# Another order of TensorE's steps in a segmented memory-transformer kernel

## The chip, the core and the metric

The kernel runs on one core of one Trainium2 chip. The metric is the device time of one execution in microseconds (us); lower is better. The core has five engines with a queue of instructions each: TensorE (PE in the profile, PEld for its loads of stationary operands), VectorE (DVE), ScalarE (ACT), GpSimd (POOL) and SyncE (SP). They run their queues in order and meet only at semaphores.

## The reference

Four layers stand one behind the other on a sequence of 2048 rows of 512 numbers: A, B, A, B, each added to its own input after a normalisation of the rows.

```
def _A_ref(x, mem0, Wq, Wk, Wv, Wo, seg_len):      # 32 heads of 128, 8 memory rows, segments of 32 rows
    mem = mem0
    for s in range(64):
        h = concatenate([mem, x[32 s : 32 s + 32]])  # 40 rows
        q, k, v = h @ Wq, h @ Wk, h @ Wv
        p = softmax(mask(q @ k.T * scale))
        o = (p @ v) @ Wo
        mem = o[:8]                                  # carried into the next segment
        outs.append(o[8:])

def _B_ref(x, wqkv, wo):                            # linear attention, 32 heads of 16
    q, k, v = x @ wqkv
    kv, z = phi(k).T @ v, sum(phi(k))
    return (phi(q) @ kv / (phi(q) @ z)) @ wo

x = x + A(layernorm(x)); x = x + B(layernorm(x))
x = x + A(layernorm(x)); x = x + B(layernorm(x))
```

Layer A is a recurrence: the eight memory rows that leave segment s enter segment s + 1, so the 64 segments of a layer can't be computed side by side. Layer B sums over all rows before any row of its result can be formed.

## The kernel before

The weights of A lie in SBUF throughout. The work is cut into 14,006 steps. A step is one call of `add` (line 1635): an engine, a function that issues one or more instructions, and the steps that it must wait for. Each step has a name made of layer, segment and part, and a count within the part, for example segment 46's `mem0`, step 5.

The parts of a segment s of layer A are these.

- `kq0`, `kq1`, `v` (function `project`, line 2125): the projections. One step of a part is one quarter of the contraction for two outputs: eight matmuls with 512 moving columns each, four at a time side by side in four column groups of TensorE. The second four use the stationary operand that the first four loaded (`again`, line 2038), so such a step is 8 matmuls and 4 weight loads. There are four steps to a part. They are the long products.
- Steps 4 to 7 of `kq0` and `kq1`: copies out of PSUM by ACT or DVE, and transposes by DVE (`turned`, line 2155).
- `mem0`, `mem1` (line 2224): the scores (steps 0 and 1 on TensorE), their exponential (ACT), two maskings (DVE), the sums (step 5, TensorE), a logarithm and an exponential (ACT), the product with v (step 8, TensorE, 20 matmuls) and the scaling (DVE), for the eight memory rows.
- `out` (lines 2373 and 2405): the output projection of the segment, eight steps of eight matmuls with 256 columns, each with its own weight load (line 2387); then a copy and an add.
- `next` (line 2410): the new memory rows are brought into the layout of the next segment, two small steps on TensorE and one copy. This closes the loop of the recurrence.
- `x` (line 2299): the attention of the 32 rows of the segment, with many small TensorE steps (step 1, steps 12 to 15 and 18 to 21); it isn't on the path of the recurrence, and runs while later segments go on.
- `res` (line 2437): moves of result rows by DMA from the queues of POOL and SP (`x_move`, line 1938) and the residual add.

Every four segments the parts `prep`, `left0`, `left1`, `leftv` and `lefts` (lines 2166 and 2207) normalise and project the rows of the next 128-row tile, and `bi` (line 2536), `bm`, `bo` and `bl` (lines 2592 and 2637) are layer B. The 512-column matmuls of `left0`, `left1`, `leftv`, `bi` and `bo` are long products too.

What sets the order is a table written out by hand, `PLACE` (lines 16 to 1558). For each part it has one number a step, and where ACT or DVE can do a step, a letter for the one that does. `when` (line 1572) reads it. `schedule` (line 1684) sorts all steps by that number and keeps the numbers for nothing else: no engine waits for a time. Each engine's queue is the sorted list of its own steps. In the same pass the eight PSUM banks are given out, always the one that became free first in that order. `finalize` (line 1721) then works out which semaphore waits each step needs in this order, and leaves out those that an earlier wait has covered already; `emit` (line 1764) writes the queues. Nothing else in the code knows of the order, so a wait on another engine, a bank and a place in a queue all follow from the table. A TensorE step that waits for two semaphores takes one instruction more.

The whole program is unrolled: TensorE runs 52,649 matmuls and 43,815 weight loads in a straight line.

Of the kernel before, what the change touches and what calls it, by code (L numbers as in the profile page):

```python
# [16 lines left out]
    (0, -9, 'setup'): '0 60 0 60 120 180 240 300 360 420 480 540 600 660 720 780 840 900 960 1020 1080 1140 120 570 1130 1690 2760 3320 3880 4440 5000 5560 6120 6680 7240 7800 8360 8920 9480 10040 10600 11160 11720 12280 12840 13400 13960 14520 15080 15640 16200 16760 17613 17295 17320 17880 18440 18993 29678a 2620 14603a 43760 19000 19560 20120 20680 21240 0 36053 18339',  # L17
    (0, -4, 'start'): '16191a',
    (0, -2, 'left0'): '25524 26387 28114 28546 29186v 30190 29185a 29827',
    (0, -2, 'left1'): '25956 28977 29409 30704 31344a 32920 31836a 32478',  # L20
    (0, -2, 'lefts'): '32862 33881 34250 38187',
    (0, -2, 'leftv'): '34490 34922 35353 35785 36425a 37066 37544 36917a 38393 40975',
    (0, -2, 'prep'): '6180 12328 12522 12855 13110 13586 15699a 15553a 15092v 15265v 14017a',
    (0, -2, 'spin4'): '19049',
    (0, 0, 'kq0'): '26819 27251 27682 29841 33131a 33773 30553v 35584',
    (0, 0, 'kq1'): '30272 31136 31567 31999 32639a 34136 34499v 35221',
    (0, 0, 'mem0'): '37080 37134 37506 38047 37907 39115 39815 40124 40228 40718',
    (0, 0, 'mem1'): '38097 38151 38523 39245 38898 40391 40829 41281 41584 41987',
    (0, 0, 'next'): '44412 44466 44731a',
    (0, 0, 'out'): '41366 41747 41965 42184 42402 42620 42839 43057 43483a 43912',  # L30
    (0, 0, 'ql'): '33624a 35947v',
    (0, 0, 'v'): '36217 36648 38251 38683 39323a 40336a',
    (0, 0, 'x'): '39038 39658 41002 41493 42244 42584 43227v 43018a 42699a 43087v 44392 44252 43707 44749 44808 44867 45828v 46417a 44353 44520 44579 44638 45316a 54737a',
    (0, 0, 'xl'): '2190',
    (0, 1, 'kq0'): '44981 45412 45844 46276 47249v 48220 46915a 47857',
    (0, 1, 'kq1'): '46707 47139 47571 48002 48642a 49783 48698v 49420',
    (0, 1, 'mem0'): '48434 48920 49292 50286 50146 50624 50967 51275 51266 51669',
    (0, 1, 'mem1'): '50315 50369 50741 51131 51271 51546 51980 52289 52279 52682',
    (0, 1, 'next'): '55082 55136 55402v',
    (0, 1, 'out'): '52061 52442 52660 52878 53097 53315 53533 53752 54178a 54606',  # L40
    (0, 1, 'ql'): '45702a 47143v',
    (0, 1, 'res'): '55089 55089',
    (0, 1, 'v'): '48488 49020 49451 49883 50524v 51488a',
    (0, 1, 'x'): '51411 51752 52502 52917 53385 53725 54285v 54005v 54145v 53865v 54947 55086 54559 54677 55190 55248 56214v 60764a 54618 54736 55360 55419 55740v 69804v',
    (0, 2, 'kq0'): '55643 56075 56506 56938 57578a 59075 58070a 58712',
    (0, 2, 'kq1'): '57370 57801 58233 58665 60045a 60687 59553a 60194',
    (0, 2, 'left0'): '32431 33449 37234 37666 38749a 39992 39385v 40355',
    (0, 2, 'left1'): '33018 34037 39226 39796 41338v 42724 41813a 43366',
    (0, 2, 'lefts'): '43766 50469 54457 56794',
    (0, 2, 'leftv'): '40503 40934 43275 43921 44824a 45465 46302 44562v 46780 51926',  # L50
    (0, 2, 'mem0'): '59528 60014 60538 61050 61189 61464 61903 62212 61835 62574',
    (0, 2, 'mem1'): '60977 61185 61678 62192 62052 62467 62787 63095 62579 63457',
    (0, 2, 'next'): '65833 65887 66153v',
    (0, 2, 'out'): '62965 63184 63402 63620 63849 64067 64285 64504 64930a 65358',
    (0, 2, 'prep'): '11720 13451 14163 14496 14752 15227 15872a 18957v 16429a 16045a 16283a',
    (0, 2, 'ql'): '52289v 56687v',
    (0, 2, 'res'): '65840 65840',
    (0, 2, 'v'): '59096 59582 60114 60545 61185a 61329v',
    (0, 2, 'x'): '62332 62742 63308 63723 64192 65698 64893v 64647v 65528a 65209a 71143 68938 66005 71729 71842 72230 73177a 76754v 71901 71959 72342 72400 73582v 77540a',
    (0, 3, 'kq0'): '66395 66827 67258 67690 68330a 69441 68331v 69078',  # L60
    (0, 3, 'kq1'): '68122 68553 68985 69417 70057v 70780 70056a 71283',
    (0, 3, 'mem0'): '69848 70334 70706 71646 71785 72118 72655 72964 72680 73326',
    (0, 3, 'mem1'): '71788 72018 72429 72944 72804 73219 73562 73871 73331 74233',
    (0, 3, 'next'): '76609 76663 76928a',
    (0, 3, 'out'): '73719 73938 74156 74374 74624 74843 75061 75279 75706a 76134',
    (0, 3, 'ql'): '65838v 64787v',
    (0, 3, 'res'): '76616 76616',
    (0, 3, 'v'): '69902 70434 70866 71297 71938v 71937a',
    (0, 3, 'x'): '73084 73493 74084 74499 74967 75842 75562v 75982v 75702v 75422v 76614 76474 76315 76374 76776 76946 81041v 81997a 76257 76433 76717 76835 77154a 81824a',
    (0, 4, 'kq0'): '77178 77609 78473 78904 79544a 80186 80037a 80678',  # L70
    (0, 4, 'kq1'): '78041 79336 79768 80199 80839a 81515 81332a 81973',
    (0, 4, 'mem0'): '81494 81548 82169 82544 82684 83539 83859 84167 83869 84529',
    (0, 4, 'mem1'): '82512 82566 82938 83431 83571 84032 84380 84689 84937 85486',
    (0, 4, 'next'): '87958 88012 88278v',
    (0, 4, 'out'): '85100 85318 85536 85755 85973 86191 86410 86628 87054a 87483',
    (0, 4, 'ql'): '74818a 76960v',
    (0, 4, 'res'): '87965 87965 82666 82884 83102 83321 83651 84144 84362 84719 85146v 85743 88535 86285 87365 86225 86795 86345 86225 88025 91895',
    (0, 4, 'v'): '80631 81063 81648 82080 83164a 82824v',
    (0, 4, 'x'): '83711 84580 84927 85342 86083 86423 86818v 86538a 87237v 87098v 86958 86678 87512 88066 88236 88295 91119a 93488a 87571 87630 87689 88125 93660a 90946a',
    (0, 4, 'xl'): '0',  # L80
    (0, 5, 'kq0'): '88519 88951 89383 89814 90454a 91169 90455v 91532',
    (0, 5, 'kq1'): '90246 90678 91109 91541 92673a 93321 92181a 92958',
    (0, 5, 'mem0'): '92836 92890 93262 93903 93763 94178 94505 94814 94805 95208',
    (0, 5, 'mem1'): '93853 93907 94279 94810 94670 95084 95519 95971 95818 96332',
    (0, 5, 'next'): '99250 99304 99570v',
    (0, 5, 'out'): '95599 96204 96422 96640 96859 97300 97519 97737 98163a 98592',
    (0, 5, 'ql'): '88384v 91062v',
    (0, 5, 'res'): '99074 99074',
    (0, 5, 'v'): '91973 92404 92990 93422 94062v 95026a',
    (0, 5, 'x'): '94949 95291 95692 96183 96929 99850 99072v 98762a 98932v 98443a 103102 105712 99790 99849 103474 104555 104876v 105464a 102066 104496 105098 106881 108481a 111020v',  # L90
    (0, 6, 'bi'): '92350 93684 94046 94678 95464 95980 92377 100491a 106074 106665 107424 107914 108866 111226 113498 120141 121449 122044 122758 123182a 133084 133601 135250 135033 121665 132861 133240 134080 134544 135457 135778 141835',
    (0, 6, 'kq0'): '99908 100339 100771 101203 101842a 103242 101843v 102566',
    (0, 6, 'kq1'): '101634 102125 102557 102988 103629v 105349 103720a 104361',
    (0, 6, 'left0'): '97955 98387 98819 99358 99998a 107934 104562a 108886',
    (0, 6, 'left1'): '105643 106992 110447 111418 112471v 119197 114791a 120975',
    (0, 6, 'lefts'): '121888 122377 126682 130721',
    (0, 6, 'leftv'): '110015 110878 117877 118471 120231a 122912 123390 122133a 123868 126635',
    (0, 6, 'mem0'): '103420 103964 104336 104724 105852 106390 107008 107316 106502 107678',
    (0, 6, 'mem1'): '105589 106290 106782 107296 107157 107640 107959 108268 107751 108630',
    (0, 6, 'next'): '111310 111364 111630v',  # L100
    (0, 6, 'out'): '108130 108348 108567 108923 109142 109360 109578 109797 110224v 110679',
    (0, 6, 'prep'): '17731 32840 37732 49518 96589 97077 97508a 99677v 101129a 100983a 102929v',
# [2630 lines left out]
```

## Time and profile before

| what | value |
| --- | --- |
| median of 3 runs | 1684.79 us (1684.59 to 1687.64) |
| the profiled execution, its own time | 1685.9 us |
| its span, first to last instruction | 1684.2 us |
| granted TensorE clock | 0.998 |
| TensorE busy | 1567.0 us (93%) |
| VectorE busy | 1229.7 us (73%) |
| ScalarE busy | 1075.6 us (64%) |

A profile row for a group of instructions gives the line of the code, the engine, the operation, what it writes and reads, how many there were, the time in which at least one ran, the mean of one, and the idle time of the engine just before them with what ended it. Four matmuls run side by side in the four column groups, and matmuls are pipelined, so the mean duration of one is far above the time by which the next four follow. In the chain of waits, pieces are given by start, length and what ran; "issue" is time in which an engine waited for nothing that the profile shows.

### The profile page before, as it was taken

To read this page: it belongs to the slowest core of one execution; us is meant where nothing else is said; L and a number is where in the kernel's file an instruction comes from. 1 tells how busy PE (TensorE), PEld (TensorE's weight loads), DVE (VectorE), ACT (ScalarE), POOL (GpSimd) and SP (SyncE) were. 2 spreads that over 40 slices of the span, in tenths; PEclk is the share of its full clock that TensorE was granted. 3 is DMA by queue.
4 is the path that set the end of the run, shared out by engine and by line. 5 is a ranking of instruction groups with operands and counts; after the bars stand their busy time and mean duration, and the time that the engine had idled before them with its cause. 6 is when DMAs were issued, how large, how long until landed. Compare 5 with 4: busy or idle time off the path is not lost.

```text
span 1684.2 us, 104983 instructions
## 1 busy us (share of the span) xinstructions
PE 1567.0 (93%) x52649; PEld 864.1 (51%) x43815; DVE 1229.7 (73%) x3944; ACT 1075.6 (64%) x2976; POOL 200.5 (12%) x406
## 2 busy tenths in 40 slices
PE   5899999999999999999999989999999999999997
PEld 1445555555555554555545545455555555555553
DVE  3667777787777777777677876777777777777777
ACT  2466666676676666666475666667666666766655
POOL 2011111101111010111101110110111111110110
PEclk9999999999999999999999999999999999999999
DMA  9200000000000000000000000000000000000004
GB/s 379 84 13 17 16 13 14 13 16 16 16 16 14 13 13 16 16 14 22 18 11 13 19 16 15 20 16 13 20 16 19 19 18 14 20 16 15 26 11 156
DMA packets 33569, 51.00 MB, mean 30 GB/s; under 512 B 10600, under 2 KB 27272, under 8 KB 31592
## 3 DMA queue, kind: packets, MB, share of 16 engines
q1 hardware_dynamic: 19288, 26.46, 4.5%
q0 software_dynamic: 13680, 17.69, 3.5%
q8 instruction: 378, 6.19, 1.6%
q14 instruction: 63, 0.52, 0.1%
q10 hardware_dynamic: 160, 0.14, 0.0%
HBM read 29.63 MB, written 10.49 MB: 24 GB/s over the span
## 4 chain that ended last, share of the span: by engine, by line
PE 78%; DVE 7%; ACT 5%; issue 4%; SPq 3%; DMA 2%; POOL 0%; DVEq 0%
PE pb L2144 24%; PE pb L2040 20%; PE pb L2387 17%; PE pb L2052 13%; ACT arena_sb L1923 3%; SPq L1954 2%; DVE arena_sb L1924 2%; PE pb L2245 1%; DMA dx_sb<-y_sb 1%; PE pb L2325 1%; DVE arena_sb L2162 1%; DVE st_sb L2084 1%; PE pb L2098 1%; DVE y_sb L2400 1%; PE pb L2418 1%
## 5 line engine op out<-in xcount | busy, mean ns | idle before, releaser
L1923 ACT ACTIVATE arena_sb<-pb 128x512 bf16<-128x512 f32 (+5 forms) x1149 | 533.7, 492 | 321.5 <-PE pb L2040 227.7
L2144 PE MATMUL pb<-Wk_sb,arena_sb 128*32 128x512 bf16 x4096 | 405.3, 380 | 8.3 <-DVE arena_sb L1924 3.9
L2040 PE MATMUL pb<-Wq_sb,arena_sb 128*32 128x512 bf16 x4096 | 404.7, 379 | 0.7 <-issue 0.6
L2387 PE MATMUL pb<-Wo_sb,arena_sb 128*32 128x256 bf16 x10368 | 358.9, 273 | 31.0 <-issue 27.1
L2052 PE MATMUL pb<-arena_sb 128*32 128x128 bf16 (+2 forms) x13808 | 366.8, 223 | 18.4 <-issue 10.5
L1924 DVE CAST arena_sb<-pb 128x512 bf16<-128x512 f32 (+3 forms) x610 | 313.8, 519 | 93.0 <-PE pb L2040 47.0
L2162 DVE STREAM_TRANSPOSE arena_sb<-arena_sb 128x256 f32<-128x256 f32 x640 | 265.3, 431 | 74.1 <-ACT arena_sb L1923 68.7
L2052 PEld LDWEIGHTS pb<-arena_sb 128*32 128x32 bf16 x13808 | 245.2, 96 | 132.4 <-issue 54.8
L2387 PEld LDWEIGHTS pb<-Wo_sb,arena_sb 128*32 128x32 bf16 x10368 | 259.2, 96 | 80.1 <-issue 49.0
L2144 PE MATMUL pb<-Wv_sb,arena_sb 128*32 128x512 bf16 x3136 | 274.9, 379 | 1.1 <-DMA Wv_sb<-in_A_Wv_dram 1.1
L2144 PEld LDWEIGHTS pb<-Wk_sb,arena_sb 128*32 128x32 bf16 x4096 | 115.9, 96 | 289.1 <-issue 216.9
L1939 POOL DMA_DIRECT2D dx_sb<-y_sb x252 | 128.3, 513 | 1043.5 <-DVE y_sb L2400 587.9
L2040 PE MATMUL pb<-Wv_sb,arena_sb 128*32 128x512 bf16 x1984 | 209.3, 379 | 0.0
L1923 ACT ACTIVATE arena_sb<-arena_sb 32x256 bf16<-32x256 bf16 (+1 forms) x382 | 142.3, 374 | 22.3 <-DVE arena_sb L2332 15.6
L2144 PEld LDWEIGHTS pb<-Wv_sb,arena_sb 128*32 128x32 bf16 x3136 | 88.2, 96 | 85.3 <-issue 24.4
L2400 DVE TENSOR_TENSOR y_sb<-pb,outW_sb 64x256 bf16<-64x256 f32 x160 | 66.7, 417 | 88.2 <-ACT outW_sb L1923 85.5
L1923 ACT ACTIVATE outW_sb<-pb 64x256 fp32r<-64x256 f32 (+1 forms) x136 | 51.1, 377 | 103.8 <-PE pb L2387 100.2
L2144 PE MATMUL pb<-Wq_sb,arena_sb 128*32 128x512 bf16 x1024 | 107.7, 378 | 4.6 <-DMA Wq_sb<-in_A_Wq_dram 2.9
L2262 ACT ACTIVATE arena_sb<-pb 128x192 bf16<-128x192 f32 (+1 forms) x256 | 84.2, 329 | 40.2 <-PE pb L2245 21.0
L2040 PE MATMUL pb<-Wk_sb,arena_sb 128*32 128x512 bf16 x1024 | 107.2, 378 | 0.4 <-issue 0.4
L2294 DVE TENSOR_TENSOR arena_sb<-pb,arena_sb 128x128 bf16<-128x128 f32 x252 | 73.1, 290 | 46.4 <-PE pb L2052 18.0
L2272 DVE TENSOR_TENSOR arena_sb<-arena_sb 128x128 bf16<-128x128 bf16 x504 | 89.1, 215 | 16.6 <-ACT arena_sb L2262 13.7
(108 smaller groups left out, 1711.9 us busy)
## 6 DMA issues: line engine op xcount, KB each, us to landing
Wk_sb<-in_A_Wk_dram SPq DMA_DIRECT2D x1, 4096.0 KB, 13.6
Wq_sb<-in_A_Wq_dram SPq DMA_DIRECT2D x1, 4096.0 KB, 24.2
Wv_sb<-in_A_Wv_dram SPq DMA_DIRECT2D x1, 4096.0 KB, 33.7
Wo_sb<-in_A_Wo_dram SPq DMA_DIRECT2D x16, 256.0 KB, 7.5
xs_scratch<-x_sb POOLq DMA_DIRECT2D x32, 128.0 KB, 2.3
pq_scratch<-arena_sb POOLq DMA_DIRECT2D x32, 128.0 KB, 2.2
arena_sb<-pq_scratch POOLq DMA_DIRECT2D x16, 128.0 KB, 2.3
x_sb<-xs_scratch POOLq DMA_DIRECT2D x16, 128.0 KB, 2.4
```

Of the source, the lines that this page charges most:

```text
L1923: return e.activation(o() if callable(o) else o, i() if callable(i) else i, ACTF.Copy)
L1924: return e.tensor_copy(o() if callable(o) else o, i() if callable(i) else i)
L1939: add(eng, lambda e: e.dma_start(o, i), 0.55 if eng == "pool" else 0.4, reads=reads, writes=writes, dsem="%s%d" % (kind, k), lat=lat + (0. ...
L2040: return pe.add_instruction(mybir.InstMatmult(name=nc.get_next_instruction_name(), engine=mybir.EngineType.PE, ins=[pe.lower_ap(x), pe.low ...
L2052: r = pe.matmul(o[q], w[:, q], x, start=start, stop=stop, skip_group_check=True, tile_position=(0, 32 * j))
L2144: r = pe.matmul(o, blk[:, c, :], w, start=(c == 0), stop=(c == 3), tile_position=(0, 32 * j))
L2162: add("dve", lambda v: v.transpose(dst, src(img[:, k, :].bitcast(F32))), 0.445, reads=[("img", k)], writes=[dkey])
L2262: add("act", lambda a: a.activation(PQ[:, r2, b, 0:nq], tl.f32()[:, 0:nq], ACTF.Exp, scale=SCALE), c_act(nq), tiles=[tl], writes=[("PQ", r ...
L2272: add("dve", lambda v, a=a, p_=p_, w_=w_: v.tensor_tensor(wide(Pm[:, k, a, :]), p_.unsqueeze(2).to_broadcast([128, 4, 4, 8]), w_, ALU.mult ...
L2294: add("dve", lambda v: v.tensor_tensor(oTb[:, s % NO, 16 * b:16 * b + 16, 0:8], pv.f32()[:, 0:128].rearrange("p (n q) -> p n q", q=8), Rm[ ...
L2387: r = pe.matmul(tl.f32()[32 * j:32 * j + 32, 0:256], oT[:, 4 * hh + n, :], Wo_sb[:, 8 * n + hh, 256 * d:256 * d + 256], start=(hh == 0 and ...
L2400: add("dve", lambda v: v.tensor_tensor(y_sb[0:64, k, :], tl.f32()[0:64, 0:256], outW[64:128, w, :].bitcast(F32), ALU.add), c_dve(256), rea ...
```

## The change

Only `PLACE` differs. Of its 14,010 numbers nearly all are other numbers, and 1169 steps have the other letter; after sorting, 4681 of TensorE's 6386 steps have another place in its queue, by at most 75 places. Measured by the TensorE work that stands ahead of a step, half of the steps move by less than 0.23 us, one in twenty by more than 0.9 us to a later place and one in twenty by more than 2 us to an earlier one. Of the `out` steps nine in ten keep their place to within 0.5 us. ACT has 15 steps fewer and DVE 15 more. The number of instructions of each kind is the same, but for the extra waits on TensorE, 324 before and 243 after.

What the reordering looks like is seen in segment 46 of the first layer. TensorE's queue there, from the last step of `kq1` on, before and after (a number in brackets is another segment):

```
before  v0  mem0_0  v1  mem0_1  v2  v3  x12(45)  mem1_0  mem1_1  x13(45)  mem0_5  left1_0  bi8  x14(45)  x15(45)  x18(45)  x19(45)  mem0_8
after   mem0_0  x12(45)  mem0_1  x13(45)  x18(45)  v0  v1  v2  x19(45)  v3  mem1_0  mem0_5  mem1_1  x14(45)  x15(45)  x20(45)  x21(45)  bi8  bi9  mem0_8
```

The `v` steps, long products, have moved behind some small steps of `x` and stand in the middle of them. Counted over the whole queue, small steps are cut by 512-column products into 896 runs, 734 before; a run has 78 instructions on average, 95 before.

The diff is 1541 lines of the table. Those of the example:

```diff
-    (0, 45, 'x'): '552853 553310 553656 554081 554549 554996 556174v 556005a 558245v 555685a 558385 557028 562497 562710 563528 563587 564086a 564993a 563698 563757 563979 564038 564491v 566157a',
...
-    (0, 46, 'kq1'): '558890 559321 559753 560185 560825v 561829 560824a 561466',
...
-    (0, 46, 'mem0'): '561048 561534 561906 562281 562420 562769 563208 563873 563816 564234',
...
-    (0, 46, 'v'): '560616 561102 561634 562065 562706v 563380a',
...
+    (0, 45, 'x'): '563597 563958 564789 564790 565255 567870 570680v 571112v 570248a 568364v 568511 568510 571751 571755 573924 573982 575135a 577469a 572393 573167 574205 574580 576159v 580850a',
...
+    (0, 46, 'kq1'): '569815 570247 570679 571110 572394a 572884 571750a 572392',
...
+    (0, 46, 'mem0'): '571750 571753 572735 573387 573247 573868 574032 574721 574723 575099',
...
+    (0, 46, 'v'): '572396 572884 572884 573226 573867v 574927a',
```

3074 rows, old and new, of the table PLACE are left out of this document.

## The prediction

> **What bounds the kernel now.** I read the page first (engines, chain, DMA queues), then TensorE's waits, then the chain around single idles.
>
> ```profile
> span 1684.2 us, 104983 instructions
> PE 1567.0 (93%) x52649; PEld 864.1 (51%) x43815; DVE 1229.7 (73%) x3944; ACT 1075.6 (64%) x2976; POOL 200.5 (12%) x406
> PEclk9999999999999999999999999999999999999999
> q8 instruction: 378, 6.19, 1.6%
> PE 78%; DVE 7%; ACT 5%; issue 4%; SPq 3%; DMA 2%; POOL 0%; DVEq 0%
> ```
>
> TensorE is the bound: 93% busy, 78% of the chain, with 0.9 or more of its clock granted in every slice. A new order can't shorten its work; it can only take out idle time. The waits of TensorE between 60 us and the end, without the start, where weights are loaded (the nine rows that end in "issue", the largest of the other twenty, and the last):
>
> ```profile
> PE pb L2387 <- issue: 26.6, 45, 1.6
> PE pb L2052 <- issue: 13.4, 24, 1.2
> PE pb L2052 <- DVE arena_sb L1924: 5.4, 12, 1.0
> PE pb L2418 <- DVE y_sb L2400: 5.3, 10, 0.9
> PE pb L2144 <- DVE arena_sb L1924: 3.9, 14, 0.9
> ...
> PE pb L2418 <- issue: 2.8, 5, 0.8
> PE pb L2560 <- issue: 2.4, 2, 1.6
> ...
> PE pb L2325 <- issue: 1.9, 2, 1.5
> PE pb L2144 <- issue: 1.7, 3, 0.7
> PE pb L2040 <- issue: 1.6, 4, 0.7
> PE pb L2194 <- issue: 1.4, 4, 0.6
> ...
> PE pb L2098 <- issue: 1.1, 1, 1.1
> ...
> PE pb L2251 <- DVE arena_sb L2162: 0.2, 1, 0.2
> ```
>
> The nine make 52.9 us in 90 idles, the other twenty 33.5 us in 78. So more is lost to no releaser at all than to every other engine together. "Issue" has a pattern. Each of these windows runs from just before the end of one such idle to just before the end of another:
>
> ```profile
> 589.47:593.04 3.57, 2.82 (x131) 2.42 (x123) 2.24 (x8) 2.22 (x8) 0.56 (x1) 1.00 0.15 41
> 1479.69:1483.43 3.74, 3.25 (x134) 2.38 (x122) 1.28 (x5) 2.45 (x7) 0.00 (x0) 1.00 0.03 7
> 969.94:973.41 3.47, 1.98 (x130) 1.70 (x126) 1.25 (x4) 0.75 (x3) 0.00 (x0) 1.00 0.02 5
> 1201.12:1204.84 3.72, 2.94 (x129) 2.62 (x126) 2.94 (x10) 1.81 (x7) 0.75 (x2) 1.00 0.03 7
> 422.54:431.33 8.79, 8.56 (x283) 4.97 (x229) 6.47 (x20) 5.74 (x15) 0.00 (x0) 1.00 0.02 5
> ```
>
> The first two counts in brackets are matmuls and weight loads: 131 + 123 = 254, 256, 256, 255, and 512 over two. Numbered through in the order of their starts, all 91 idles of this kind in the trace end at instruction 193 or 194 of a block of 256. The queue q8 has 378 packets, and (52,649 + 43,815) / 378 = 255: a packet is a block of TensorE's instructions. So TensorE stands still at the end of a block when the next one isn't there yet, and two neighbouring blocks can't begin closer than about 3.6 us (3.47 to 3.74), though a packet itself takes 1.6% x 16 x 1684.2 / 378 = 1.14 us. Such a block in the chain of waits:
>
> ```profile
> 1478.52 1.18 issue
> 1479.70 0.29 PE pb L2052 x12
> ...
> 1480.04 0.37 PE pb L2052 x36
> ...
> 1481.21 1.09 PE pb L2387 x40
> 1482.31 0.22 PE pb L2144 x4
> 1482.52 0.22 PE pb L2040 x4
> ...
> 1482.95 0.49 issue
> ```
>
> To last 3.6 us a block needs 14.1 ns an instruction. A projection step (four matmuls with loads, four without) takes 0.22 + 0.22 us for 12 instructions, 36 ns each. The output projection takes 1.09 us for 40 matmuls and 40 loads, 13.6 ns. The small products of `x` take 0.37 us for 72, 5.1 ns. A block full of `x` and `out` steps empties too soon; with a few projection steps among them it doesn't. The mean block lasts 1684.2 / 378 = 4.46 us, so evenly mixed no block would fall short.
>
> **The change part by part.** *The idle at block ends.* An idle shows in the trace only from the modelled end of the last matmul. This row
>
> ```profile
> L2387 PE MATMUL pb<-Wo_sb,arena_sb 128*32 128x256 bf16 x10368 | 358.9, 273 | 31.0 <-issue 27.1
> ```
>
> has 273 ns for a matmul, while the next four follow after 1.09 / 10 = 0.109 us; 0.164 us of each idle is hidden. The loss is 52.9 + 90 x 0.164 = 67.7 us. Adding up, step by step, by how much each start is later than such steps usually follow gives 67 us at the block ends as well.
>
> For the new order I sorted the two tables, wrote down TensorE's instructions with the extra waits, cut them into blocks at the same phase, and gave each step its usual spacing in this trace. Blocks with less than 3.6 us of work: 191 before, 179 after; less than 2.8 us: 110 and 77; less than 2.4 us: 54 and 28. Not every short block costs an idle: in the order before, the bare sum of what is missing to 3.6 us is 180 us and the measured loss 67.7. Instructions already drawn from a block ahead of their execution give time. So I set the loss of a block to what is missing to L in its 256 instructions and d more before them (none after an idle), and chose L with d so that the order before gives what was measured:
> - d = 56, L = 3.55 us: 69 us before (102 blocks over 0.15 us), 17 us after (37). This pair follows the measured losses block by block best (correlation 0.68).
> - d = 16, L = 3.10 us: 69 us before (113 blocks), 36 us after (69); correlation 0.57.
>
> I take the better-fitting pair: 67.7 - 17, about **50 us less**. Bounds: 32 less (36 left) and 68 less (none left). A loss in this part is excluded by the counts, which fall in every class.
>
> *Waits on other engines.* The new order puts some products nearer behind what feeds them. For each TensorE step that waits, I followed the awaited instruction back to the TensorE step before it, added the durations in between, from rows such as these (ACT copies, DVE transposes and adds)
>
> ```profile
> L1923 ACT ACTIVATE arena_sb<-pb 128x512 bf16<-128x512 f32 (+5 forms) x1149 | 533.7, 492 | 321.5 <-PE pb L2040 227.7
> L2162 DVE STREAM_TRANSPOSE arena_sb<-arena_sb 128x256 f32<-128x256 f32 x640 | 265.3, 431 | 74.1 <-ACT arena_sb L1923 68.7
> L2400 DVE TENSOR_TENSOR y_sb<-pb,outW_sb 64x256 bf16<-64x256 f32 x160 | 66.7, 417 | 88.2 <-ACT outW_sb L1923 85.5
> ```
>
> and compared with the TensorE work that the order leaves between. Before, 126 chains fall short by more than 0.1 us, 49.5 us in all; measured are 33.5 + 78 x 0.164 = 46.3 us, so this count is about the right size. After, it is 185 chains and 65.9 us: 16 us more. Lower end: 0, if the new ones ripen in the shadow of other waits, since a wait that TensorE takes anyway gives every other chain time. Upper end: 59 new ones at the mean of a visible idle, 33.5 / 78 = 0.43 us, 25 us. I take the middle, **13 us more**. What is queued behind such a wait is all of TensorE; that is why it counts in full.
>
> *ACT and DVE.* 15 steps go from ACT to DVE, by the mean rows 15 x 0.5 us = 7.5 us on an engine that is idle for 454 us: nothing, unless they stand on one of the chains just counted.
>
> *DMA issues.* On POOL's queue 236 of 402 steps change places, on SP's 141 of 296; most are the row moves of `res`. Queues run ahead of TensorE, so what matters is whether an issue stands behind one that still waits: 185 do before, 196 after. No add or projection gets a DMA as its last wait that didn't have one (45 and 46 cases, nearly all the residual adds). POOL is 12% busy. Nothing, and 2 us (one landing) if one case is late.
>
> *Extra wait instructions* fall by 81, a third of a block: at 3.6 us a block about 1 us, left out. The start (weight loads) and the end keep their TensorE work to 1 us; nothing.
>
> Sum against the profiled execution: 1685.9 - 50 + 13 = 1648.9 us; it stood 1.1 us over the median, so **1648 us**. The ends: 1684.8 - 68 + 0 = 1617, and 1684.8 - 32 + 25 + 2 = 1680.
>
> **The rivals.**
> 1. *Forecast*, block ends mostly filled, a few more waits: 1648, own range 1618 to 1674. Chance 0.75.
> 2. *All of it*: no block runs dry and the waits stay in shadows: 1617. For it: the mean block is well over 3.6 us. Against: 179 blocks are still under it. Chance 0.13.
> 3. *Slower*: long products now stand in front of steps of the recurrence, whose loop crosses TensorE at every `mem`, `out` and `next`. A projection step in front of one of them costs up to 0.43 us in each of 126 segments, 54 us; from 0.40 us a segment on, it eats the 50 us. With two such a segment: 1685 - 50 + 108 = 1743. For it: 59 more short chains. Against: nine in ten `out` steps keep their place to 0.5 us, and the count finds 16 us, not 50. Chance 0.07.
> 4. *No effect*: the idle isn't a matter of which instructions fill a block, so it only moves to other steps: 1685. Against: the windows above, always 256 and always about 3.6 us apart. Chance 0.05.
>
> [...]
>
> **How the numbers follow.** Likeliest is the first, 1648. The range must leave out no more than 2 in 10: 1616 to 1674 holds nearly all of the first and most of the second, and leaves out the third and fourth. Faster by over 0.2% (3.4 us, about what a measurement of this kernel can tell from no change): 0.74 of the first, 0.13, and 0.01 of the fourth, 0.88. Within 0.2%: 0.03 of the fourth. Slower: the third, 0.01 of the first and of the fourth, 0.09.
>
> **What would show it.** TensorE's "issue" rows after 60 us fall from 52.9 us in 90 idles to some 10 to 30 us, and the idles left still end 256 instructions apart. The rows with DVE and ACT as releasers rise from 33.5 to 40 to 60 us. TensorE's busy time and q8's packets stay. I am wrong if "issue" stays above 40 us, or if waits on DVE or ACT rise by more than 50 us, with L2144, L2245 or L2418 as the waiting lines; then the recurrence has become the bound.

## The result and the profile after

The changed kernel takes 1656.39 us (median of 4 runs, 1654.92 to 1657.94) where the kernel before takes 1685.59 (4 runs, 1684.59 to 1687.64): a ratio of 0.9825, with a 95% interval of 0.9808 to 0.9842. That is 29 us less; 1648 was forecast, in a range of 1616 to 1674. The profiled execution took 1656.06 us, 29.8 less than that of before.

The page of the changed kernel (span, engines, the instruction queue, the chain of waits by engine, and the group of the output projection):

```profile
span 1654.1 us, 104914 instructions
PE 1561.4 (94%) x52649; PEld 846.3 (51%) x43815; DVE 1230.1 (74%) x3959; ACT 1065.6 (64%) x2961; POOL 200.8 (12%) x406
q8 instruction: 377, 6.18, 1.6%
PE 72%; DVE 12%; ACT 6%; issue 3%; DMA 3%; SPq 3%; POOL 0%; DVEq 0%; ACTq 0%
L2387 PE MATMUL pb<-Wo_sb,arena_sb 128*32 128x256 bf16 x10368 | 350.9, 273 | 12.7 <-issue 10.7
```

The work is the same: the same 52,649 matmuls and 43,815 weight loads, a packet less in the instruction queue q8. Idle time ahead of the output projection went from 31.0 to 12.7 us. In the chain, "issue" fell from 4% to 3%, but DVE rose from 7% to 12%: part of the gain was paid for with waits on other engines. TensorE's waits of the changed kernel from 60 us to the end (all seven rows that end in "issue", and the largest of the others; columns: total us, times, longest us):

```profile
PE pb L2418 <- DVE y_sb L2400: 9.3, 24, 0.9
PE pb L2052 <- DVE arena_sb L1924: 8.7, 19, 1.1
PE pb L2387 <- issue: 7.7, 20, 0.8
PE pb L2052 <- issue: 6.4, 10, 2.1
PE pb L2052 <- DVE arena_sb L2272: 4.2, 14, 0.6
...
PE pb L2098 <- issue: 2.5, 3, 1.1
...
PE pb L2052 <- DMA arena_sb<-pq_scratch: 2.3, 1, 2.3
PE pb L2040 <- issue: 2.2, 4, 1.0
...
PE pb L2245 <- issue: 1.0, 2, 0.7
...
PE pb L2560 <- issue: 0.6, 1, 0.6
...
PE pb L2194 <- issue: 0.5, 1, 0.5
```

The seven sum to 20.9 us in 41 idles, against 52.9 in 90. All other rows together are 42.2 us in 100, against 33.5 in 78. The idles left without a releaser are still block ends. Windows of the changed kernel from just before the end of one such idle to just before the end of another (length, then PE and PEld with their counts):

```profile
918.80:926.54 7.74, 7.19 (x275) 4.46 (x236) 4.93 (x20) 6.04 (x17) 1.56 (x3) 1.00 0.10 26
1264.22:1268.24 4.02, 3.42 (x138) 1.99 (x118) 3.22 (x10) 2.26 (x7) 0.00 (x0) 1.00 0.06 19
1628.87:1632.99 4.12, 2.85 (x127) 2.25 (x127) 3.19 (x6) 3.41 (x7) 0.46 (x1) 1.00 0.11 36
```

275 + 236 is 511, two blocks of 256 less one record; 138 + 118 is 256; 127 + 127 is 254. Numbered through as in the prediction, all 42 idles of this kind in the whole trace end at instruction 193 to 195 of a block. Two neighbouring idles 256 instructions apart lie 4.0 and 4.1 us from each other in these windows. In all there are four such pairs here, 3.72 to 4.11 us apart, and ten in the trace of before, 3.47 to 3.75.

The packets of the queue q8 in the traces show what these idles wait for. With the packets set beside the blocks in order, each of the 91 idles before ends 1.22 to 1.60 us after the packet of its block has landed, and each of the 42 idles of the changed kernel 1.27 to 1.72 us after it. No block in either trace begins sooner than 1.22 us after its packet, and the blocks without an idle often begin much later: of 377 blocks, 122 before and 106 after begin over 3 us after theirs. So the idle at a block end is a wait for the next packet of instructions. The prediction's limit of about 3.6 us between blocks is one between packets: before, no two packets begin closer than 3.23 us (4.00 in the median), while 105 of the 377 distances between block starts are under 3.4 us, the least 1.89.

For finer accounts than the visible idles, I took for every TensorE step after 60 us the distance to the start of the next one, less the median of that distance for steps of its shape in the trace of before, and summed it apart for steps on a block end and for all others. It counts the hidden part of an idle too, and small spread, so its differences are what is read. Before: 86.8 us at block ends and 75.5 elsewhere. After: 39.1 and 93.0. That is -47.7 and +17.5, together -30.2, against 29.8 between the two profiled executions.

### The profile page after: what moved, and what is told of

Same layout as the page of the kernel before. It is cut to its first block, busy times and chain, and to the rows that moved or that the text cites. A ratio compares the mean times of both kernels' runs of the same rounds, so it can differ in the third digit from the quotient of the medians.

```text
span 1654.1 us, 104914 instructions
## 1 busy us (share of the span) xinstructions
PE 1561.4 (94%) x52649; PEld 846.3 (51%) x43815; DVE 1230.1 (74%) x3959; ACT 1065.6 (64%) x2961; POOL 200.8 (12%) x406
## 4 chain that ended last, share of the span: by engine, by line
PE 72%; DVE 12%; ACT 6%; issue 3%; DMA 3%; SPq 3%; POOL 0%; DVEq 0%; ACTq 0%
PE pb L2144 22%; PE pb L2040 19%; PE pb L2387 15%; PE pb L2052 12%; ACT arena_sb L1923 3%; DVE arena_sb L1924 3%; SPq L1954 2%; DMA dx_sb<-y_sb 2%; DVE arena_sb L2162 2%; PE pb L2245 1%; DVE y_sb L2400 1%; DVE st_sb L2084 1%; PE pb L2098 1%; PE pb L2325 1%; PE pb L2418 1%
## 5 line engine op out<-in xcount | busy, mean ns | idle before, releaser
L1923 ACT ACTIVATE arena_sb<-pb 128x512 bf16<-128x512 f32 (+6 forms) x1155 | 533.0, 491 | 312.1 <-PE pb L2040 195.7
L2040 PE MATMUL pb<-Wq_sb,arena_sb 128*32 128x512 bf16 x4096 | 404.0, 379 | 0.4 <-issue 0.4
L2052 PE MATMUL pb<-arena_sb 128*32 128x128 bf16 (+2 forms) x13808 | 380.5, 222 | 19.7 <-DVE arena_sb L1924 8.9
L2387 PE MATMUL pb<-Wo_sb,arena_sb 128*32 128x256 bf16 x10368 | 350.9, 273 | 12.7 <-issue 10.7
L2052 PEld LDWEIGHTS pb<-arena_sb 128*32 128x32 bf16 x13808 | 244.9, 95 | 164.6 <-issue 46.9
L2387 PEld LDWEIGHTS pb<-Wo_sb,arena_sb 128*32 128x32 bf16 x10368 | 256.8, 96 | 60.4 <-issue 24.3
L1923 ACT ACTIVATE outW_sb<-pb 64x256 fp32r<-64x256 f32 (+1 forms) x124 | 46.3, 375 | 94.3 <-PE pb L2387 93.2
L2144 PE MATMUL pb<-Wq_sb,arena_sb 128*32 128x512 bf16 x1024 | 103.1, 382 | 2.3 <-DMA Wq_sb<-in_A_Wq_dram 2.2
## 6 DMA issues: line engine op xcount, KB each, us to landing
Wk_sb<-in_A_Wk_dram SPq DMA_DIRECT2D x1, 4096.0 KB, 13.5
```

The lines of the kernel that those rows point to most:

```text
L1923: return e.activation(o() if callable(o) else o, i() if callable(i) else i, ACTF.Copy)
L2040: return pe.add_instruction(mybir.InstMatmult(name=nc.get_next_instruction_name(), engine=mybir.EngineType.PE, ins=[pe.lower_ap(x), pe.low ...
L2052: r = pe.matmul(o[q], w[:, q], x, start=start, stop=stop, skip_group_check=True, tile_position=(0, 32 * j))
L2144: r = pe.matmul(o, blk[:, c, :], w, start=(c == 0), stop=(c == 3), tile_position=(0, 32 * j))
L2387: r = pe.matmul(tl.f32()[32 * j:32 * j + 32, 0:256], oT[:, 4 * hh + n, :], Wo_sb[:, 8 * n + hh, 256 * d:256 * d + 256], start=(hh == 0 and ...
```

## The experiments

None of them changes what is computed: the orders hold the same steps, and the filler products write to a tile that nobody reads. Ratios are to the kernel before on the same chip. One table holds what the sections use. The count is that of the prediction (what the 256 instructions of a block, with d more before them, lack of L), here with d = 40 and L = 3.35 us, a pair chosen after the first six runs, so that it fits the shifts among them; the last two rows were counted with it ahead of their runs.

| kernel | ratio | visible "issue", us in idles | other waits, us in idles | block ends by starts | elsewhere by starts | counted |
| --- | --- | --- | --- | --- | --- | --- |
| before | 1 | 52.9 in 90 | 33.5 in 78 | 86.8 | 75.5 | 68.9 |
| changed | 0.9825 | 20.9 in 41 | 42.2 in 100 | 39.1 | 93.0 | 22.4 |
| changed, 96 loads ahead | 0.9937 | 32.4 in 67 | 41.5 in 100 | 59.6 | 92.3 | 43.8 |
| before, 96 loads ahead | 1.0052 | 61.4 in 98 | 28.8 in 83 | 89.6 | 81.6 | 75.1 |
| changed, 48 loads ahead | 0.9836 | 13.5 in 32 | 43.0 in 100 | 29.4 | 98.7 | 24.2 |
| changed, letters of before | 1.0373 | 6.8 in 18 | 113.1 in 248 | 31.6 | 192.1 | about 18 |
| before, letters of the changed | 1.0227 | 35.5 in 54 | 71.9 in 156 | 63.6 | 134.1 | about 73 |
| third order | 0.9783 | 16.7 in 34 | 36.3 in 87 | 34.9 | 89.2 | 12.1 |
| third order, 96 loads ahead | 0.9943 | 36.4 in 70 | 33.6 in 86 | 57.4 | 90.6 | 52.8 |

### Another phase of the blocks

If block ends decide, then the same order must take another time when its block ends fall on other steps. 96 more weight loads in a stretch of filler products at the start move every later instruction by 96 places within its block, and nothing else. The edit, in the changed kernel and, the same, in the kernel before:

```diff
-    SPIN = {..., (0, 4): (30, 512, 10)}
+    SPIN = {..., (0, 4): (30, 512, 106)}
```

> The changed kernel with 96 more weight loads in the block of filler products at the start (they reload what is loaded and run beside the 512-column matmuls there), so that every later block of 256 TensorE instructions ends 96 instructions earlier in the work. Nothing else moves. Theory 1 (idle at the ends of blocks, and the new order is laid out for its own block ends): the count of the prediction gives 47 us of block losses in place of 17, so 20 to 30 us slower than the changed kernel, about 1675 to 1686, nearly all of the gain gone, with the idles 256 apart as ever. Theory 2 (the gain comes from the mixing as such, wherever the blocks end): within 5 us of the changed kernel.

> The kernel before with the same 96 more weight loads at the start. Theory 1: the order before is at its block ends little better than elsewhere; the count gives 77 us in place of 69, so 0 to 10 us slower, 1685 to 1696. Theory 2: no change, 1685. The pair of shifted kernels shows how much of the change is left when neither order is at its own phase: 0 to 15 us by theory 1, 30 us by theory 2.

The changed kernel took 1674.64 us with the shift, the kernel before 1692.94, and the unaltered kernel before 1686.56 on that chip: ratios 0.9937 (0.9915 to 0.9959) and 1.0052 (1.0034 to 1.0069). So a shift that alters no wait cost the changed kernel 0.9937 - 0.9825 = 1.1%, 18 to 19 us, a little less than the 20 to 30 of theory 1. Its waits:

```profile
PE pb L2387 <- issue: 21.0, 41, 1.3
PE pb L2418 <- DVE y_sb L2400: 8.7, 21, 0.9
PE pb L2052 <- DVE arena_sb L1924: 8.5, 17, 0.9
PE pb L2052 <- issue: 8.2, 19, 0.9
```

The two rows on DVE stand as they were (9.3 and 8.7); the idle ahead of L2387 went from 7.7 us in 20 to 21.0 in 41. By starts, block ends went from 39.1 to 59.6 and the rest stayed. So the time depends on where the block ends fall. With both orders shifted, the changed one is 1692.94 - 1674.64 = 18.3 us ahead, more than the 0 to 15 of theory 1 and less than the 30 of theory 2. By starts it has 30.0 us less at block ends there and 10.7 more elsewhere. The other 11 or so of the 29 us go with the phase. The kernel before was run at these two phases alone, so what the mixing is worth in the mean over all phases stays open.

### Half of that shift

With 48 loads more instead of 96 (`(30, 512, 58)`), the two pairs of lead and block time differ.

> As the changed kernel shifted by 96, but by 48 weight loads. The count gives 32 us of block losses there, half way between 17 at its own block ends and 47 at 96. Theory 1: half of the 18 us that the shift by 96 cost, 6 to 12 us slower than the changed kernel, 1662 to 1668. If the 18 us came from the added loads themselves or from anything at the start: less than 2 us of difference in the losses at block ends, or the same 18 us as with 96.

It took 1653.15 us, a ratio of 0.9836 (0.9811 to 0.9861), which isn't told apart from the unshifted 0.9825: added loads by themselves cost nothing that shows. I had expected a loss of 6 to 12 us by the lead of 56 instructions; that lead is refuted. With d = 40 and L = 3.35 us the count gives +1.8 us for this shift, +21.4 for the shift by 96, and +6.2 for the kernel before, where about +2, +18 to 19 and +6 to 9 were measured. The pair was chosen to fit these, so that is no test of it, and it misses the parts: by starts, this shift took 9.7 us off the block ends (39.1 to 29.4) and put 5.7 on elsewhere. The prediction's other pair, d = 16 and L = 3.10 us, counts some 15 us less at block ends for this shift, but only some 8 more for the shift by 96. No pair tried has both.

### A dense stretch

The block time can be measured by itself, in a stretch with nothing else: in the changed kernel, the filler products between the two layers become 1140 matmuls of 128 columns more, each of the 1168 with its own weight load, 2304 instructions or nine blocks in all.

```diff
-    SPIN = {..., (0, 3): (7,), ...}
+    SPIN = {..., (0, 3): (292, 128, 1164), ...}
```

> The changed kernel in which the seven filler products of 512 columns, which stand ahead of the first use of layer B's result, are replaced by 292 filler products of 128 columns (1168 matmuls, each with its own weight load, 2304 instructions more: nine blocks, so that all later block ends stay where they are). It measures the disputed cost by itself: nothing in this stretch waits on another engine. By the spacing of such products elsewhere (0.055 us for four matmuls and four loads) it takes 292 x 0.055 = 16 us. Theory 1 (blocks of 256 instructions arrive no closer than about 3.6 us): 9.1 blocks x 3.5 to 3.7 us = 32 to 34 us, one idle of 1.5 to 1.9 us in each block, kernel 30 to 33 us slower than the changed one. Rival (blocks arrive ahead and the idles have another cause, such as the other engines' use of the weights or of PSUM at those places): 16 us without idles, kernel 14 to 15 us slower.

One execution took 1682.85 us, where the changed kernel stands at about 0.9825 x 1679.73 = 1650 on that chip: 32 us more, inside the 30 to 33 of theory 1; the rival had 14 to 15. The chain of waits through the stretch (start, length, what ran):

```profile
816.18 1.51 PE pb L2067 x108
817.69 1.22 issue
818.91 1.97 PE pb L2067 x128
820.88 2.05 issue
822.93 1.97 PE pb L2067 x128
824.90 1.78 issue
...
834.18 1.97 PE pb L2067 x128
836.15 2.05 issue
838.21 2.57 PE pb L2067 x128
840.78 1.19 issue
841.96 5.80 PE pb L2067 x256
847.76 1.15 issue
```

Each run of 128 matmuls, which with its 128 loads is one block, is done in 1.97 us, and then TensorE stands for 1.2 to 2.05 us, with no other engine in between. The block starts from 818.91 to 841.96 are six distances, 4.02, 3.75, 3.48, 4.02, 4.03 and 3.75 us: 3.84 us in the mean. So fast did blocks come here, slower than both times of the counts, 3.55 and 3.35 us, and not evenly: the distance varies by over half a microsecond. The packets of q8 show its parts. There are six in these six blocks, each for the block that follows: the packet began 1.05 to 1.62 us after the block before it had begun, took 0.93 to 1.49 us, and TensorE went on 1.28 to 1.51 us after it had landed. In this stretch no packet was ahead by more than one block. Of the 23.05 us of the six distances, TensorE stood for 10.62, nearly half.

### The letters

1169 steps also changed between ACT and DVE, which the prediction costed at nothing. Two kernels take the numbers of one table with the letters of the other. One line of the first (the changed kernel with the old letters), and one of the second:

```diff
-    (0, 0, 'kq1'): '27112 29271 30997 31584 32224a 32866 33592a 36921',
+    (0, 0, 'kq1'): '27112 29271 30997 31584 32224a 32866 33592v 36921',
...
-    (0, 46, 'kq1'): '558890 559321 559753 560185 560825v 561829 560824a 561466',
+    (0, 46, 'kq1'): '558890 559321 559753 560185 560825a 561829 560824a 561466',
```

> The new order of all steps, but each step that ACT or DVE can do goes to the engine that did it before (1169 letters undone). Theory 1 (TensorE's order is the change): the block losses stay (20 us by the count, 17 with the new letters), short chains 184 against 185, so 1650 to 1665. Theory 3 (the new split of copies between ACT and DVE carries a good part of the gain or of the new waits): more than 8 us away from 1656 to either side.

> The old order of all steps with the new letters, the other half of the change alone. Theory 1: block losses 76 us by the count against 69, short chains 128 against 126, so 1683 to 1697. Theory 3: well under 1680.

Both fell far outside: 1746.84 us (ratio 1.0373, 1.0352 to 1.0394) and 1721.37 us (1.0227, 1.0201 to 1.0253). Waits of the first:

```profile
PE pb L2251 <- DVE arena_sb L2162: 14.8, 32, 1.3
PE pb L2052 <- DVE arena_sb L1924: 14.7, 24, 1.3
PE pb L2418 <- DVE y_sb L2400: 14.2, 27, 1.3
PE pb L2052 <- DVE arena_sb L2272: 12.7, 35, 0.7
PE pb L2052 <- ACT arena_sb L1923: 11.6, 22, 1.4
...
PE pb L2387 <- issue: 3.4, 9, 0.8
```

The loss is in waits on other engines, 113.1 us in place of 42.2, all but 1.5 of them on ACT and DVE. Block ends cost less than in the changed kernel (6.8 us visible in place of 20.9; by starts 31.6 in place of 39.1). That blocks arrive while TensorE waits for something else would explain this, but it wasn't tested. So the new order is no better by itself: with the old letters it is 60 us slower than the order before. Orders and letters fit only in the pairs in which they came, in both tables. The letters change TensorE's extra waits as well (282 in the first and 259 in the second, where the whole tables have 243 and 324), and so move block ends a little. My count of short chains gave 184 for the first and 128 for the second, nearly what it gives for the two whole tables (185 and 126); it follows one chain at a time and doesn't see the step that stands ahead in the queue of the same engine.

### A third order

If block ends and waits are the two prices, an order that is lower in both should be faster than the changed kernel. A third table of the same steps, in which 582 letters differ from the changed kernel's as well, for instance (beside the line of the changed kernel, the end of both left out)

```diff
-    (0, 45, 'x'): '563597 563958 564789 564790 565255 567870 570680v 571112v 570248a ...',
+    (0, 45, 'x'): '487200 488400 488800 489400 491500 491300 491900v 491700a 493200a ...',
```

was run beside the changed kernel, then once more for a second profile, and then with the 96 loads ahead.

> A third order of the same operations (every matmul, transfer and ACT or DVE step as before; only the strings of PLACE and some letters differ), chosen so that both counts are lower at once. Counted with a lead of 40 instructions and 3.35 us of work per block of 256 PE instructions, what the blocks lack is 68.9 us for the old order, 22.4 for the new one and 12.1 for this one; the counts of chains through ACT and DVE that are shorter than their work are 126 with 49.5 us, 185 with 65.9 us, and 152 with 56.7 us. Theory 1 (two prices: the distance of blocks, and waits on other engines): 10 us less at block ends and 5 to 9 less in waits, so 12 to 20 us under the changed kernel, a ratio to the kernel before of 0.971 to 0.976, that is 1636 to 1645 us where the kernel before takes 1685; visible idle with no releaser falls from 20.9 us to 10 to 15, other waits from 42.2 to 33 to 38. Rival (what the changed kernel has left is the spread of block arrivals and chains that the counts don't see, as with the exchanged letters): within 4 us of the changed kernel, ratio 0.980 to 0.985, or above it when the counted chains miss the queues again.

> The changed kernel unaltered, beside the third order on the same chip, so that the two are compared with the same runs of the kernel before. Both theories: ratio 0.9825 within 0.002.

> The third order once more, for its own profile: in the profiled execution of the first time it took 1652.86 us against 1642.35 to 1645.55 in the other four, so that profile can't show where the gain lies. Theory 1 (two prices): ratio 0.978 within 0.002 again, and in a profile of a usual execution the visible idle with no releaser is at 10 to 15 us and other waits at 33 to 37. Rival (the gain lies elsewhere than at block ends): the same ratio with 18 to 21 us of idle with no releaser.

> The third order with 96 more weight loads in the first stretch of filler products, as the two shifts before. Counted with a lead of 40 and 3.35 us a block, the block losses go from 12.1 to 52.8 us; the chains through the other engines are untouched. Theory 1: by the first shift, where 21.4 counted came out as 18, 30 to 40 us over the third order, a ratio to the kernel before of 0.996 to 1.002. Rival (the third order's gain is not at block ends): within 10 us of the third order, ratio below 0.985.

It took 1644.31 us (ratio 0.9779, 0.9754 to 0.9805) beside 1654.16 of the changed kernel (0.9829, 0.9807 to 0.9851), and 1645.86 (0.9783, 0.9765 to 0.9801) the second time: about 9 us faster than the changed kernel, and the fastest of all here. Theory 1 had asked for 12 to 20, its rival for less than 4; neither had the size. The waits of the second profile (1646.34 us):

```profile
PE pb L2052 <- issue: 9.5, 17, 1.2
PE pb L2418 <- DVE y_sb L2400: 8.6, 18, 1.7
PE pb L2387 <- issue: 6.3, 15, 0.8
PE pb L2052 <- DVE arena_sb L1924: 5.0, 15, 0.8
```

"Issue" in all stands at 16.7 us in 34 idles and the other waits at 36.3 in 87; by starts, 4.2 us came off at block ends and 3.8 elsewhere, where the counts had 10.3 and 9. With the 96 loads ahead it took 1671.91 us, 26 more than without (counted: 40.7; expected: 30 to 40), 22.5 of them at block ends by starts; the waits on other engines stayed:

```profile
PE pb L2387 <- issue: 13.8, 28, 1.0
PE pb L2052 <- issue: 8.3, 17, 1.4
PE pb L2418 <- DVE y_sb L2400: 7.5, 15, 1.3
```

So the third order's advantage holds at its own phase and is fragile: shifted alike, it isn't told apart from the changed kernel (0.9943, 0.9929 to 0.9958, and 0.9937, 0.9915 to 0.9959). At its own phase only half of the 8 us seen by starts is at block ends. The count has the sign of these steps right and their size 1.6 to 2.5 times too large. What it leaves out, I take to be the varying arrival of the blocks, by which an order that is just long enough on the mean still runs dry at times; that was argued from the six distances of the dense stretch and not tested by itself.

## Why the prediction was right, point by point

- **The bound and the cause of "issue".** Right. The idles left are 256 instructions apart, a shift of the phase alone moves the time by 19 us, a stretch of nothing but small products runs at 3.84 us a block, and every such idle of the two kernels ends 1.2 to 1.7 us after the landing of its block's packet. That two blocks can't begin closer than 3.6 us was wrong as it was put: block starts come as close as 1.89 us, packets no closer than 3.23. The fourth rival (no effect, 1685 us) is refuted for this kernel.
- **The term of the block ends.** The forecast was 50 us less, from 67.7 to 17. Measured in the same manner, 20.9 + 41 x 0.164 = 27.6 us are left, 40 us less; by starts it is 47.7. The term was too large by 2 to 10 us, and the step that failed is the choice of the lead of 56 instructions with 3.55 us: the half shift refutes it. The lower bound, 32, held. The 27.6 us that remain lie between the 17 and the 36 of the two pairs; which count would give them stays open, and the uneven arrival of the packets speaks against any single block time.
- **The waits on other engines.** 13 us more were forecast, from a count that gave 16. The visible waits and 0.164 for each went from 46.3 to 42.2 + 100 x 0.164 = 58.6 us, 12.3 more; by starts 17.5. Right in size. The rows that grew are adds of `y_sb` in front of L2418 (5.3 to 9.3) and casts in front of L2052 (5.4 to 8.7).
- **ACT and DVE.** "Nothing" held for the sum of the two tables, but the reason given, 15 steps of 0.5 us, was no reason: the choice of the engine for the 1169 steps is worth 90 us in the new order (1746.84 against 1656.39) and 35 to 38 in the old one. They couldn't be costed by how many steps each engine got; it was luck that the pair fitted.
- **DMA.** Nothing was forecast, or 2 us if one landing is late. One is: the 2.3 us on `pq_scratch`, which has no row before.
- **The extra wait instructions and busy time.** q8 lost one packet. TensorE's busy time was to stay and fell by 5.6 us, though the work is the same. Busy time holds the hidden part of each idle: 49 fewer block ends and 22 more other waits make (49 - 22) x 0.164 = 4.4 us of it.
- **The sum.** -50 + 13 = -37 us was forecast; 27.6 - 67.7 + 12.3 = -28 is what the same terms measure, and -29 the median. The forecast is 8 us low. By the visible idles all of that comes from the block ends; by starts, 2.3 us of the miss lie there and 4.5 elsewhere. The range was cut at 1674, although the slow end of the sum itself was 1680; the time fell well inside both.
- **The slower rival** (long products in front of the recurrence, 1743 us) didn't come. The 1747 us with the old letters aren't its case, near as the figure is: the order of TensorE's steps is the new one in both, and what grew are waits on ACT and DVE by the choice of engine. No run tested long products in front of the recurrence by themselves.

## What to carry to other kernels

Where TensorE is busy all the time and the profile still shows idle without a releaser, number its instructions through, and set the packets of the instruction queue beside them. Here the idles ended at instruction 193 to 195 of a block of 256, 1.22 to 1.72 us after the block's packet had landed, so the stream of instructions was the limit there. In the dense stretch blocks came 3.48 to 4.03 us apart, so by an estimate from these distances 256 matmuls, loads and waits together needed some 3.5 to 4.0 us of work, about 15 ns each. Mix long products into stretches of small ones: the order that does so lost 39.1 us at block ends by starts here, the one before 86.8. Part of such a gain belongs to the phase at which the blocks fall and can be lost by an edit that adds instructions ahead (96 loads lost 18 us here, 48 none), so a new order is to be judged at more than one phase. An order and the assignment of its helper steps to ACT and DVE are one thing: change them together, or measure them together.

## What the runs showed of the hardware that was not expected

In the dense stretch the granted clock fell. The windows of that kernel (length, PE and PEld with counts, the other engines, then PEclk):

```profile
816.00:818.90 2.90, 1.69 (x112) 1.55 (x105) 1.77 (x3) 1.61 (x3) 0.54 (x1) 1.00 0.16 51
818.90:838.20 19.30, 9.85 (x640) 9.12 (x640) 0.00 (x0) 0.00 (x0) 1.07 (x2) 1.00 0.06 18
838.20:849.00 10.80, 8.46 (x392) 8.03 (x395) 0.00 (x0) 0.00 (x0) 0.00 (x0) 0.68 0.02 5
```

After 19.3 us in which TensorE was busy for 9.85, with idles of at most 2.05 us, the clock stood at 0.68 in the mean of the next 10.8 us (0.50 from 839.4 to 846.2 us, then 1.00 again), and 128 matmuls took 2.57 us instead of 1.97. What set it off wasn't tested. The stretch lost nothing by it that shows: the two blocks after 841.96 lasted 6.95 us, 3.48 each, no longer than those before.

The second was the width of the blocks' arrival, 3.48 to 4.03 us in one stretch: the packets took 0.93 to 1.49 us and didn't always begin equally soon.
